# A pair's attention scores as two 64-row products, with the mask from a standing tile

## The chip, the cores and the metric

The kernel runs on one core of one Trainium2 chip. The time is device microseconds of one execution, the median of three runs: 210.06 us before the change (209.74 to 210.12). Everything said about single instructions comes from one profiled execution.

## What is computed

Block-sparse attention over 4 batches, 8 heads, 768 positions and 64 features, followed by a gated MLP with a spatial product. The change touches the attention alone:

```python
scores = scale * np.matmul(q, k.transpose(0, 1, 3, 2))
...
scores = np.where(mask, scores, -1000000000.0)
scores = scores - np.max(scores, axis=-1, keepdims=True)
attn = np.exp(scores)
attn = attn / (np.sum(attn, axis=-1, keepdims=True) + 1e-09)
return np.matmul(attn, v).astype(np.float32)
```

The mask is one 768 x 768 pattern of 32 x 32 blocks, the same for all heads and batches: a band, the first and last block of rows and columns, and three sampled blocks for each block of rows.

## The kernel before

Heads are worked on in pairs: a batch has four pairs, the kernel 16 (`p`). A pair's keys and queries are cast to bf16 by GpSimd (`nat`), and a DMA transpose on SP's queue (`tr_dma`, L372) turns them into `tt`, 128 partitions by 12 blocks of 128 columns: partitions 0 to 63 hold the features of the pair's first head, 64 to 127 those of its second; the first six blocks are keys, the other six queries. The first batch (pairs 0 to 3) is transposed on TensorE instead and has its own functions.

`kq` (L83) has a row of 2 x 768 columns for each of eight heads. Its partitions 0 to 63 are that head's keys and queries. Its partitions 64 to 127 are the mask, written once: on the key side a one-hot of the key's block, on the query side 0 for an allowed block and -300 for a forbidden one. One product over all 128 partitions therefore gives score plus mask. VectorE copies each head of `tt` into its row of `kq` (`split`, L376), two copies for a pair.

From batch 1 on, the work goes by slots. A unit `j` is one head; it has six slots, one for each chunk `ci` of 128 keys. In a slot `qk_full` (L422) makes the scores of 128 keys by all 768 queries in two matmuls (512 and 256 columns) into one of two score buffers of PSUM (`sc`, two banks each), and ScalarE writes their exponential into `a_all`. Seven slots later (`LAG`) `av_full` (L471) multiplies: for one chunk `qc` of 128 queries, six matmuls of 65 columns over the six chunks of keys; the 65th column is the sum. When a unit's six are done, VectorE normalises it into `xn` (`normalize`, L438). In between, each slot takes some steps of the MLP off a queue (`run_queue`): matmuls of up to 512 columns into two single PSUM banks (`moeA`, `moeB`), read by VectorE or ScalarE. The order on each engine is the order in which the program issues; the slot lists `at`, `pre` and `late` say what else is issued in a slot, and the main loop (L846) runs scores, `pre`, value products, `at`, MLP steps, `late`. Slots 0 to 35 (`S0` = 36) are the first batch, slots 36 to 179 the 24 units of the other three.

Before the loop, `mask_rows` (L268) makes the mask's query side with a product of `bm`, in one case over partitions 64 to 87 alone; the matmuls of `filler` (L177) stand around it.

Of the kernel before, what the change touches and what calls it, by code (L numbers as in the profile page):

```python
# [10 lines left out]
FP32 = mybir.dt.float32  # L11
BF16 = mybir.dt.bfloat16
I32 = mybir.dt.int32
AF = mybir.ActivationFunctionType
ALU = mybir.AluOpType
# [11 lines left out]
def kernel(  # L27
# [16 lines left out]
    nc = tc.nc  # L44

    B, H, S, D = q.shape
# [3 lines left out]
    NCH = S // 128  # L50
# [6 lines left out]
    NG = H // 2  # L57
# [13 lines left out]
    work = ctx.enter_context(tc.tile_pool(name="work", bufs=1))  # L71
    psum = ctx.enter_context(tc.tile_pool(name="psum", bufs=1, space=bass.MemoryType.PSUM))
# [10 lines left out]
    kq = const.tile([128, H, 2 * S], BF16, name="kq")  # L83
# [2 lines left out]
    MR = slice(D, KR)  # L86
    MX = slice(D, 128)
    K_, Q_ = slice(0, S), slice(S, 2 * S)

    def qcols(t0, n=1):  # L90
        return slice(S + t0 * TW, S + (t0 + n) * TW)
# [91 lines left out]
    def ts(out, in0, s1, o0, s2=None, o1=None):  # L183
        kw = {} if o1 is None else {"op1": o1}
        nc.vector.tensor_scalar(out=out, in0=in0, scalar1=s1, scalar2=s2, op0=o0, **kw)  # L185

    def tt_op(out, in0, in1, op):
        nc.vector.tensor_tensor(out=out, in0=in0, in1=in1, op=op)
# [21 lines left out]
    def dve_copy(o, i):  # L210
        nc.vector.tensor_copy(out=o, in_=i)  # L211
# [158 lines left out]
    tt = {}  # L370

    def tr_dma(p):  # L372
        tt[p] = work.tile([128, 2 * NCH, 128], BF16, tag="tt", bufs=2, name="tt")
        nc.sync.dma_start_transpose(out=tt[p], in_=nat.pop(p).rearrange("p c h d -> p (c h d)"))

    def split(p, h):  # L376
        src = tt[p].rearrange("x c n -> x (c n)")
        dve_copy(kq[0:D, (2 * p + h) % H, :], src[h * D:(h + 1) * D, :])


    a_ref, av_ref, x_ref, xn_ref, xt_ref = {}, {}, {}, {}, {}

# [4 lines left out]
    def qk_unit(u, e):  # L387
# [31 lines left out]
            ps = ps.rearrange("p (c n) -> p c n", c=len(parts))  # L419
        nc.scalar.activation(out=out, in_=ps, func=AF.Exp, scale=0.125)  # L420

    def qk_full(j, ci):  # L422
        if ci == 0:
            a_ref["h", j] = work.tile([128, NCH * S], BF16, tag="a_all", bufs=3,
                                      name="a_all").rearrange("p (c n) -> p c n", c=NCH)
        ps = psum.tile([128, 1024], FP32, tag="sc", bufs=2)
        for n0, n1 in ((0, 512), (512, S)):
            nc.tensor.matmul(out=ps[:, n0:n1],  # L428
                             lhsT=kq[:, j % H, ci * 128:(ci + 1) * 128],
                             rhs=kq[:, j % H, S + n0:S + n1], start=True, stop=True)  # L430
        nc.scalar.activation(out=a_ref["h", j][:, ci, :], in_=ps[:, 0:S], func=AF.Exp, scale=0.125)  # L431

    def av_tile(key, n):
        ps = psum.tile([128, 512], FP32, tag="av", bufs=2, name="ps_av")
        av_ref[key] = ps[:, 0:n * VA].rearrange("p (c d) -> p c d", d=VA)
        x_ref[key] = ps[:, 512 - TW // 2:512].bitcast(BF16)

    def normalize(ps, out, n):  # L438
        rc = work.tile([128, NCH, 1], FP32, tag="rc", bufs=2)
        nc.vector.reciprocal(out=rc[:, 0:n], in_=ps[:, :, D:VA])  # L440
        nc.vector.tensor_tensor(out=out, in0=ps[:, :, 0:D],  # L441
                                in1=rc[:, 0:n].to_broadcast([128, n, D]), op=ALU.mult)

    def av_unit(u, e):
        t, p = UNITS[u]
        if e == 0:
            av_tile(u, 2 * TC)
        for i in range(8 * e, 8 * e + 8):
            g, ci = divmod(i, NCH)
            if t == "h":  # L450
                h, qc, to, n = p, g, g, 2 * TC
                pp = 0
            else:
                (h, qc), n, pp = divmod(g, TC), TC, p
                to = qc * 2 + h
            at = (h * NCH + ci) * n * 128 if t != "h" else ci * n * 128
            at += qc * 128
            nc.tensor.matmul(out=av_ref[u][:, to, :], lhsT=a_ref[u][:, at:at + 128],  # L458
                             rhs=vv[pp % NVV][:, h, ci, :],
                             start=(ci == 0), stop=(ci == NCH - 1))  # L460
        if e == 2:
            a_ref.pop(u)
            if t == "h":
                if p == 0:
                    xn_ref[0] = work.tile([128, 2 * TC, 2, D], BF16, tag="xn0", bufs=1, name="xn0")
                normalize(av_ref.pop(u), xn_ref[0][:, :, p, :], 2 * TC)
            else:
                xn_ref[u] = work.tile([128, TC, 2, D], BF16, tag="xn3", bufs=3, name="xn3")
                normalize(av_ref.pop(u), xn_ref[u].rearrange("p c h d -> p (c h) d"), 2 * TC)

    def av_full(j, qc):  # L471
        p, h = divmod(j, 2)
        if qc == 0:
            av_tile(j, NCH)
        for ci in range(NCH):
            nc.tensor.matmul(out=av_ref[j][:, qc, :],  # L476
                             lhsT=a_ref["h", j][:, ci, qc * 128:(qc + 1) * 128],
                             rhs=vv[p % NVV][:, h, ci, :],
                             start=(ci == 0), stop=(ci == NCH - 1))
        if qc == NCH - 1:  # L480
            a_ref.pop(("h", j))
            if h == 0:
                xn_ref["p", p] = work.tile([128, NCH, 2, D], BF16, tag="xn", bufs=2, name="xn")
            normalize(av_ref.pop(j), xn_ref["p", p][:, :, h, :], NCH)

    def xt_tile(p):
        if p not in xt_ref:
# [224 lines left out]
    def run_queue():  # L712
        if not queue or pace["slots"] <= 0:
            return
        pace["credit"] += (len(queue) - pace["credit"]) / pace["slots"]
        pace["slots"] -= 1
        n = int(pace["credit"] + 0.5)
        for _ in range(min(n, len(queue))):
            queue.popleft()()
            pace["credit"] -= 1  # L720
# [3 lines left out]
    at, late, pre = {}, {}, {}  # L724

    def when(slot, *fns):
        at.setdefault(slot, []).extend(fns)

    def c(f, *a, **kw):
        return lambda: f(*a, **kw)  # L730
# [77 lines left out]
    def slot_of(p):  # L808
        return S0 + 12 * (p - NG)

    for p in range(NG, NP):
        g = slot_of(p)
        when({4: 14, 5: 20, 6: 28, 11: g - 29, 15: g - 29}.get(p, g - 36), c(load, p, "k"), c(load, p, "q"), c(load, p, "v"))
        when({4: 17, 5: 23, 6: 37, 11: g - 22, 15: g - 22}.get(p, g - 24),
             *[c(cast, p, nm, PL, cs=cs) for nm in "kqv" for cs in (((C01, C23, C45) if p > 5 else (ALLC,)))])
        when({4: 21, 5: 27, 11: g - 18, 15: g - 18, 10: g - 17, 14: g - 17}.get(p, g - 19), c(tr_dma, p))
        if p % NG == 1 and p > 2 * NG:
            late.setdefault(g - 4, []).append(c(split, p, 0))
        else:
            when(g - 5, c(split, p, 0))  # L820
        when(g + 4 if p == NG else g - 3, c(split, p, 1))
        if p == NP - 1:
            when(g + 20, last_x)
        elif p % NG == NG - 1:
            when(g + 19, c(xtr_dma, p))
        else:
            when(g + 20, c(xtr_dma, p))
# [13 lines left out]
    for u in range(len(UNITS)):  # L841
        for e in range(3):
            sl = (5, 6, 6)[e] if u == 0 else 3 * u + e + (4 if u < 3 else 3)
            av_at.setdefault(sl, []).append((u, e))
    NS = S0 + 12 * (NP - NG)
    for s in range(NS + LAG + 2):  # L846
        if s < S0:
            qk_unit(*divmod(s, 3))
        elif s < NS:
            j, ci = divmod(s - S0, NCH)  # L850
            qk_full(j + H, ci)
        early = at.get(s, [])
        for f in pre.get(s, []):
            f()
        for u, e in av_at.get(s, []):
            av_unit(u, e)
        if 0 <= s - LAG - S0 and s - LAG < NS:
            j, qc = divmod(s - LAG - S0, NCH)
            av_full(j + H, qc)
        for f in early:  # L860
            f()
        run_queue()
        for f in late.get(s, []):
            f()
        while post:
            post.pop(0)()
# [31 lines left out]
```

## Time and profile before

| | |
|---|---|
| time, median of 3 runs | 210.06 us |
| span of the profiled execution | 208.3 us |
| TensorE, matmul busy | 201.0 us (97%) |
| TensorE, weight loads | 138.0 us (66%) |
| VectorE busy | 146.8 us (70%) |
| ScalarE busy | 168.4 us (81%) |
| GpSimd busy | 89.4 us (43%) |
| granted TensorE clock | 1.000 |

The span runs from the first to the last instruction of that execution; the time holds in addition what lies around it. PE is TensorE's matmuls, PEld its weight loads, DVE VectorE, ACT ScalarE, POOL GpSimd, SP the engine that issues the transfers. In a row of instruction groups stand the line, the engine, the operation, what is written and read with partitions x elements, the count, the busy time, the mean of one in ns, and the idle time of the engine just before, with what ended it. A row of the order of time has start, length (both us) and how many instructions are merged. Matmuls are pipelined: a row's length includes the way through the array, so the pace is read from the distance between starts.

### The profile page before, as it was taken

To read this page: it belongs to the slowest core of one execution; us is meant where nothing else is said; L and a number is where in the kernel's file an instruction comes from. 1 tells how busy PE (TensorE), PEld (TensorE's weight loads), DVE (VectorE), ACT (ScalarE), POOL (GpSimd) and SP (SyncE) were. 2 spreads that over 40 slices of the span, in tenths; PEclk is the share of its full clock that TensorE was granted. 3 is DMA by queue.
4 is the path that set the end of the run, shared out by engine and by line. 5 is a ranking of instruction groups with operands and counts; after the bars stand their busy time and mean duration, and the time that the engine had idled before them with its cause. 6 is when DMAs were issued, how large, how long until landed. Compare 5 with 4: busy or idle time off the path is not lost.

```text
span 208.3 us, 5489 instructions
## 1 busy us (share of the span) xinstructions
PE 201.0 (97%) x2203; PEld 138.0 (66%) x2225; DVE 146.8 (70%) x315; ACT 168.4 (81%) x222; POOL 89.4 (43%) x186
## 2 busy tenths in 40 slices
PE   6899999999999999999999999999999999999993
PEld 6599888777766776667556676667665567445551
DVE  6888776989876766575975585456875666576871
ACT  6899999999999999989899878889899884266021
POOL 6888989767927964006757600006210000013000
PEclk9999999999999999999999999999999999999999
DMA  5999899999999999499987920499402010610016
GB/s 143 338 362 357 275 383 270 206 247 389 253 253 308 259 300 208 139 199 386 292 176 206 139 41 0 164 189 335 75 0 41 0 37 4 250 57 0 0 70 232
DMA packets 53053, 39.48 MB, mean 190 GB/s; under 512 B 33956, under 2 KB 47652, under 8 KB 53028
## 3 DMA queue, kind: packets, MB, share of 16 engines
q1 hardware_dynamic: 52596, 38.74, 70.0%
q10 hardware_dynamic: 432, 0.39, 0.6%
q8 instruction: 17, 0.28, 0.5%
q14 instruction: 8, 0.07, 0.1%
HBM read 24.77 MB, written 6.29 MB: 149 GB/s over the span
## 4 chain that ended last, share of the span: by engine, by line
PE 87%; DVE 4%; ACT 4%; DMA 2%; issue 1%; POOL 0%; ACTq 0%
PE ps L428 21%; PE ps_moe L630 17%; PE ps_moe L561 13%; PE ps_av L476 12%; PE ps L415 7%; PE ps_av L458 4%; PE ps_t L561 4%; PE ps_t L630 4%; PE ps_sc L630 2%; ACT a_all L420 2%; DVE stats L594 2%; DVE vn L185 2%; DMA st_q<-in_q_dram 2%; PE ps_sc L561 1%; PE ps L263 1%
## 5 line engine op out<-in xcount | busy, mean ns | idle before, releaser
L431 ACT ACTIVATE a_all<-ps 128x768 bf16<-128x768 f32 x144 | 113.4, 812 | 13.8 <-PE ps L428 6.2
L428 PE MATMUL ps<-kq 128*128 128x512 bf16 (+1 forms) x288 | 70.3, 326 | 0.3
L476 PEld LDWEIGHTS <-a_all 128*128 128x128 bf16 x864 | 46.6, 98 | 19.0
L476 PE MATMUL ps_av<-vv,a_all 128*128 128x65 bf16 x864 | 51.1, 194 | 0.1
L428 PEld LDWEIGHTS <-kq 128*128 128x128 bf16 x288 | 27.9, 97 | 23.6
L137 POOL CAST nat<-st_k 128x256 bf16<-128x256 f32 (+3 forms) x37 | 17.7, 509 | 38.7 <-DMA st_k<-in_k_dram 38.7
L420 ACT ACTIVATE a_all<-ps 128x1024 bf16<-128x1024 f32 x35 | 33.5, 1027 | 0.3
L630 PE MATMUL ps_moe<-w_spt,vn 128*128 128x512 bf16 (+1 forms) x144 | 33.1, 325 | 0.0
L598 POOL TENSOR_SCALAR std<-mv 128x3 f32<-128x3 f32 (+1 forms) x9 | 3.4, 376 | 48.7 <-DVE mv L595 48.5
L661 DVE TENSOR_TENSOR sb<-ps_moe,b_row 128x512 f32<-128x512 f32 x18 | 12.4, 690 | 14.5 <-PE ps_moe L630 14.2
L630 PE MATMUL ps_moe<-xt,w_in_t 128*128 128x256 bf16 (+1 forms) x108 | 21.7, 299 | 0.2
L415 PE MATMUL ps<-kq 128*128 128x256 bf16 x135 | 20.8, 275 | 0.8 <-DVE kq L211 0.6
L561 PE MATMUL ps_moe<-w_in_t,xt 128*128 128x512 bf16 x65 | 20.2, 378 | 0.2
L137 POOL CAST vv<-st_v 128x256 bf16<-128x256 f32 (+2 forms) x37 | 18.5, 533 | 3.9 <-DMA st_v<-in_v_dram 3.8
L137 POOL CAST nat<-st_q 128x256 bf16<-128x256 f32 (+2 forms) x41 | 19.2, 496 | 1.6 <-DMA st_q<-in_q_dram 1.5
L561 PE MATMUL ps_moe<-w_out_t,un 128*128 128x512 bf16 x64 | 19.4, 378 | 0.2
L441 DVE TENSOR_TENSOR xn<-ps_av,rc 128x384 bf16<-128x384 f32 (+1 forms) x36 | 18.5, 513 | 1.4 <-DVE rc L440 0.2
L664 DVE TENSOR_TENSOR un<-sb,un 128x512 bf16<-128x512 f32 x24 | 17.4, 727 | 1.5
L630 PEld LDWEIGHTS <-vn 128*128 128x128 bf16 x192 | 15.5, 97 | 4.4
L594 DVE BATCH_NORM_STATS2 stats<-vn 128x6 f32<-128x512 bf16 x24 | 16.5, 688 | 1.5 <-ACT vn L589 0.9
L211 DVE COPY osb<-ps_moe 128x512 f32<-128x512 f32 x12 | 8.3, 689 | 11.2 <-PE ps_moe L561 9.3
L211 DVE COPY kq<-tt 64x1536 bf16<-64x1536 bf16 x24 | 15.4, 641 | 0.6 <-DMA tt<-nat 0.2
(94 smaller groups left out, 241.6 us busy)
## 6 DMA issues: line engine op xcount, KB each, us to landing
out_dram<-osb SPq DMA_DIRECT2D x23, 256.0 KB, 2.1
st_k<-in_k_dram SPq DMA_DIRECT2D x15, 384.0 KB, 4.6
st_v<-in_v_dram SPq DMA_DIRECT2D x15, 384.0 KB, 6.2
st_q<-in_q_dram SPq DMA_DIRECT2D x12, 384.0 KB, 4.9
ws_f<-in_moe_w_spatial_dram SPq DMA_DIRECT2D x6, 384.0 KB, 5.5
w_f<-in_moe_w_in_dram SPq DMA_DIRECT2D x8, 256.0 KB, 6.3
w_f<-in_moe_w_out_dram SPq DMA_DIRECT2D x4, 256.0 KB, 5.4
st_q<-in_q_dram SPq DMA_DIRECT2D x3, 256.0 KB, 6.9
```

Of the source, the lines that this page charges most:

```text
L137: eng.tensor_copy(out=dst, in_=src)
L211: nc.vector.tensor_copy(out=o, in_=i)
L415: nc.tensor.matmul(out=ps[:, at:at + n * TW], lhsT=kq[:, h, ci * 128:(ci + 1) * 128], rhs=kq[:, h, qcols(t0, n)], start=True, stop=True)
L420: nc.scalar.activation(out=out, in_=ps, func=AF.Exp, scale=0.125)
L428: nc.tensor.matmul(out=ps[:, n0:n1], lhsT=kq[:, j % H, ci * 128:(ci + 1) * 128], rhs=kq[:, j % H, S + n0:S + n1], start=True, stop=True)
L431: nc.scalar.activation(out=a_ref["h", j][:, ci, :], in_=ps[:, 0:S], func=AF.Exp, scale=0.125)
L441: nc.vector.tensor_tensor(out=out, in0=ps[:, :, 0:D], in1=rc[:, 0:n].to_broadcast([128, n, D]), op=ALU.mult)
L476: nc.tensor.matmul(out=av_ref[j][:, qc, :], lhsT=a_ref["h", j][:, ci, qc * 128:(qc + 1) * 128], rhs=vv[p % NVV][:, h, ci, :], start=(ci == ...
L561: nc.tensor.matmul(out=ref["ps"][:, 0:w], lhsT=lhs(i), rhs=rhs(i), start=(i == 0), stop=(i == n - 1))
L594: nc.vector.bn_stats(out=stats, in_=self.vn[:, tcc, :])
L630: nc.tensor.matmul(out=o.rearrange("p (c t) -> p c t", c=n), lhsT=lhs(i)[:, (d0 + x) * 128:(d0 + x + 1) * 128], rhs=rhs(i), start=(i == 0) ...
L664: nc.vector.tensor_tensor(out=self.in_place(*area), in0=sb, in1=self.in_place(*area), op=ALU.mult)
```

## The change

A unit `j` is no longer one head with all queries but a pair `p` with half `f` of the queries, 384 of them. For a chunk of 128 keys the two heads' scores are two products, each over 64 partitions, straight from `tt`: partitions 0 to 63 into the first bank of the score buffer, 64 to 127 into the second. The copies of `split` are gone. From pair 6 on, `tt` is not a tile of its own but row 4 + (p - 2) % 4 of `kq`.

The mask comes in two ways. For four chunks of keys (0, 2, 4, 5) two more 64-row products add it to the scores in PSUM, from row 0 of `kq`, whose lower half `mask_low` fills with a copy of its upper half. For chunks 1 and 3 (`DVE_MASKED`) the exponential is taken of the plain scores, and VectorE then takes the minimum with `keep`, which is 0 where the mask forbids and 3e38 where it allows. `keep` stands in rows 1 to 3 of `kq`; `mask_chunk` makes two of its chunks in slots 30 and 31, by a pair of 64-row products and a comparison.

```diff
+    keep = kq[:, 1:4].rearrange("p h n -> p (h n)").rearrange("p (c n) -> p c n", c=NCH)
+    TOP = 3.0e38
...
     def tr_dma(p):
-        tt[p] = work.tile([128, 2 * NCH, 128], BF16, tag="tt", bufs=2, name="tt")
+        if p < NG + 2:
+            tt[p] = work.tile([128, 2 * NCH, 128], BF16, tag="tt", bufs=2, name="tt")
+        else:
+            tt[p] = kq[:, 4 + (p - 2) % 4].rearrange("x (c n) -> x c n", n=128)
...
-    def split(p, h):
-        src = tt[p].rearrange("x c n -> x (c n)")
-        dve_copy(kq[0:D, (2 * p + h) % H, :], src[h * D:(h + 1) * D, :])
...
+    DVE_MASKED = (1, 3)
+    HW = S // 2
+
+    def mask_low():
+        dve_copy(kq[0:D, 0, :], kq[MX, 0, :])
+
+    def mask_chunk(ci):
+        ps = psum.tile([128, 1024], FP32, tag="sc", bufs=2, name="ps_m").rearrange("p (h n) -> p h n", h=2)[:, :, 0:HW]
+        for f in range(2):
+            r = slice(f * D, (f + 1) * D)
+            nc.tensor.matmul(out=ps[:, f], lhsT=kq[r, 0, ci * 128:(ci + 1) * 128],
+                             rhs=kq[r, 0, S + f * HW:S + (f + 1) * HW], start=True, stop=True)
+        ts(keep[:, ci].rearrange("p (f n) -> p f n", f=2), ps, -1.0, ALU.is_ge, TOP, ALU.mult)
+
     def qk_full(j, ci):
+        p, f = divmod(j, 2)
...
-        ps = psum.tile([128, 1024], FP32, tag="sc", bufs=2)
-        for n0, n1 in ((0, 512), (512, S)):
-            nc.tensor.matmul(out=ps[:, n0:n1],
-                             lhsT=kq[:, j % H, ci * 128:(ci + 1) * 128],
-                             rhs=kq[:, j % H, S + n0:S + n1], start=True, stop=True)
-        nc.scalar.activation(out=a_ref["h", j][:, ci, :], in_=ps[:, 0:S], func=AF.Exp, scale=0.125)
+        ps = psum.tile([128, 1024], FP32, tag="sc", bufs=2, name="ps_s").rearrange("p (h n) -> p h n", h=2)[:, :, 0:HW]
+        by_dve = ci in DVE_MASKED
+        for h in range(2):
+            r = slice(h * D, (h + 1) * D)
+            nc.tensor.matmul(out=ps[:, h], lhsT=tt[p][r, ci], rhs=tt[p][r, NCH + f * TW3:NCH + (f + 1) * TW3],
+                             start=True, stop=by_dve)
+        if not by_dve:
+            for h in range(2):
+                r = slice(h * D, (h + 1) * D)
+                nc.tensor.matmul(out=ps[:, h], lhsT=kq[r, 0, ci * 128:(ci + 1) * 128],
+                                 rhs=kq[r, 0, S + f * HW:S + (f + 1) * HW], start=False, stop=True)
+        a = a_ref["h", j][:, ci]
+        nc.scalar.activation(out=a, in_=ps, func=AF.Exp, scale=0.125)
+        if by_dve:
+            masks.append(lambda: tt_op(a, a, keep[:, ci:ci + 1, f * HW:(f + 1) * HW].to_broadcast([128, 2, HW]), ALU.min))
...
     def av_full(j, qc):
...
-                             lhsT=a_ref["h", j][:, ci, qc * 128:(qc + 1) * 128],
+                             lhsT=a_ref["h", j][:, ci, h, ql * 128:(ql + 1) * 128],
...
+    when(30, mask_low)
+    for i, ci in enumerate(DVE_MASKED):
+        late.setdefault(30 + i, []).append(c(mask_chunk, ci))
...
             av_full(j + H, qc)
+        while masks:
+            masks.pop(0)()
```

`av_full` takes the value products of a unit by half of the queries and by head (`ql, h = divmod(qc, 2)`); their number and size stay. The order of the DMA issues, of the casts on GpSimd and of the exponentials on ScalarE stays as it was.

More of the change, by code (lines that the diff above doesn't have):

```diff
@@ L422, in qk_full @@
     def qk_full(j, ci):
+        p, f = divmod(j, 2)
         if ci == 0:
             a_ref["h", j] = work.tile([128, NCH * S], BF16, tag="a_all", bufs=3,
-                                      name="a_all").rearrange("p (c n) -> p c n", c=NCH)
-        ps = psum.tile([128, 1024], FP32, tag="sc", bufs=2)
-        for n0, n1 in ((0, 512), (512, S)):
-            nc.tensor.matmul(out=ps[:, n0:n1],
-                             lhsT=kq[:, j % H, ci * 128:(ci + 1) * 128],
-                             rhs=kq[:, j % H, S + n0:S + n1], start=True, stop=True)
@@ L431, in qk_full @@
-        nc.scalar.activation(out=a_ref["h", j][:, ci, :], in_=ps[:, 0:S], func=AF.Exp, scale=0.125)
+                                      name="a_all").rearrange("p (c h n) -> p c h n", c=NCH, h=2)
+        ps = psum.tile([128, 1024], FP32, tag="sc", bufs=2, name="ps_s").rearrange("p (h n) -> p h n", h=2)[:, :, 0:HW]
[4 more added lines that the diff above has]
+                             start=True, stop=by_dve)
@@ L433, in av_tile @@
+        if ci == NCH - 1 and f == 1:
+            tt.pop(p)
+    masks = []
+    TW3 = NCH // 2
     def av_tile(key, n):
@@ L471, in av_full @@
     def av_full(j, qc):
-        p, h = divmod(j, 2)
+        p, f = divmod(j, 2)
+        ql, h = divmod(qc, 2)
         if qc == 0:
@@ L481, in av_full @@
             a_ref.pop(("h", j))
-            if h == 0:
+            if f == 0:
                 xn_ref["p", p] = work.tile([128, NCH, 2, D], BF16, tag="xn", bufs=2, name="xn")
-            normalize(av_ref.pop(j), xn_ref["p", p][:, :, h, :], NCH)
+            normalize(av_ref.pop(j), xn_ref["p", p][:, f * TW3:(f + 1) * TW3].rearrange("p c h d -> p (c h) d"), NCH)
     def xt_tile(p):
@@ L816 @@
         when({4: 21, 5: 27, 11: g - 18, 15: g - 18, 10: g - 17, 14: g - 17}.get(p, g - 19), c(tr_dma, p))
[L817 to L821, printed above, removed]
         if p == NP - 1:
```

## Prediction

> **What bounds the kernel now.** I read the shares of busy time first, then the chain of work that ended last, then the costliest groups.
>
> ```profile
> span 208.3 us, 5489 instructions
> PE 201.0 (97%) x2203; PEld 138.0 (66%) x2225; DVE 146.8 (70%) x315; ACT 168.4 (81%) x222; POOL 89.4 (43%) x186
> ...
> PE 87%; DVE 4%; ACT 4%; DMA 2%; issue 1%; POOL 0%; ACTq 0%
> ...
> L431 ACT ACTIVATE a_all<-ps 128x768 bf16<-128x768 f32 x144 | 113.4, 812 | 13.8 <-PE ps L428 6.2
> L428 PE MATMUL ps<-kq 128*128 128x512 bf16 (+1 forms) x288 | 70.3, 326 | 0.3
> ```
>
> TensorE is busy 97% of the span and is 87% of the chain. A busy matmul row includes the end of its pipeline, so the 97% alone proves little; the 0.3 us of idle time before 288 score matmuls says more: TensorE practically never waits. Next I asked for the busy time in the stretch where the changed function runs (first score matmul of L428 to the last exponential), and in the part of it where VectorE is fullest.
>
> ```profile
> core 0: us, PE busy (x) PEld busy (x) DVE busy (x) ACT busy (x) POOL busy (x), PEclk, DMA share, GB/s
> 40.30:173.00 132.70, 131.95 (x1456) 87.74 (x1469) 92.18 (x181) 119.02 (x159) 51.74 (x113) 1.00 0.75 185
> ...
> 36.00:52.00 16.00, 15.89 (x191) 11.69 (x190) 14.67 (x33) 15.22 (x19) 11.73 (x23) 1.00 1.12 284
> ```
>
> 144 chunks (24 units of six) take 132.7 us, 0.92 us each. TensorE sets this pace; ScalarE with 119.0 us is 13.7 us behind it, VectorE with 92.2 us further. What TensorE gains or loses per chunk is therefore gained or lost at the end, down to ScalarE's floor. The third view is the order of time on TensorE and its weight loads, to see what one chunk is made of.
>
> ```profile
> 104.18 0.38 PE L561 MATMUL ps_moe<-w_in_t,xt 128*128 128x512 bf16 x1
> 104.39 0.49 PE L428 MATMUL ps<-kq 128*128 128x512 bf16 x2
> 104.72 0.35 PE L476 MATMUL ps_av<-vv,a_all 128*128 128x65 bf16 x6
> 104.91 0.59 PE L561 MATMUL ps_moe<-w_in_t,xt 128*128 128x512 bf16 x2
> 105.34 0.49 PE L428 MATMUL ps<-kq 128*128 128x512 bf16 x2
> ...
> 104.18 0.31 PEld L428 LDWEIGHTS <-kq 128*128 128x128 bf16 x2
> ```
>
> Read starts, not lengths. Two 512-column matmuls go from 104.91 to 105.34: 0.215 us each, 0.42 ns a column. The scores (512 + 256 columns) hold TensorE for 0.32 us, the six value products for 0.19 us, 0.032 us each. The first score weights were loaded from 104.18 on, beside the matmul before: loads cost nothing here as long as they may run ahead.
>
> **The change on TensorE, columns.** A chunk had 768 columns on the whole array. Now it has a pair of 64-row products of 384 columns each, one on partitions 0 to 63, one on 64 to 127, into two banks of PSUM; four chunks of six have a second such pair for the mask. No row of this trace shows two matmuls at once, so the pair is bounded: at best both halves stream together, 384 columns, 0.16 us; at worst one after the other, 0.32 us. I take together, because the two share no partition, no row of the array and no bank, with the second product starting half of the 0.032 us pitch later (0 to 0.032). An unmasked chunk then takes 0.16 + 0.016 instead of 0.32 us, −0.145; a chunk with mask 0.32 + 0.016, +0.016. A unit: 2 × −0.145 + 4 × 0.016 = −0.226 us; 24 units: **−5.4 us** (−7.7 with no offset, −3.1 with 0.032; one after the other, 0 for two chunks and +0.32 for four, +31 us). The Trainium skill, "TensorE: Matmul & The Clock Gate", section "The mechanism" of part 3, says that matmuls on different row groups run at the same time, about 4 ns apart; by that the term would be −7.1 us, and no run here shows it.
>
> **The change on TensorE, going between whole array and half.** The stream around each score pair stays on 128 rows. The trace has one matmul that uses less than half of the rows, the mask product of L269 with 24 rows at partition 64:
>
> ```profile
> 5.14 0.28 PE L179 MATMUL wps<-warm 128*128 128x128 bf16 x2
> ...
> 5.19 0.22 PE L179 MATMUL wps<-warm 128*128 128x128 bf16 x1
> 5.34 0.28 PE L269 MATMUL mq<-kq,bm 24*128 24x256 bf16 x1
> ...
> 5.08 0.15 PEld L179 LDWEIGHTS <-warm 128*128 128x128 bf16 x2
> 5.34 0.09 PEld L269 LDWEIGHTS <-bm 24*128 24x128 bf16 x1
> ...
> 3.46 0.84 ACT L214 ACTIVATE kq<-kq 64x768 bf16<-64x768 bf16 x1
> 3.74 0.17 DVE L185 TENSOR_SCALAR bm<-allow 24x24 bf16<-24x24 f32 x1
> ```
>
> The two fillers ahead of it start at 5.14 and 5.19, 0.055 us apart, so the next matmul was due at 5.25. It started at 5.34, and its weight load, which elsewhere starts beside the matmul before, started at 5.34 too, though `bm` had been ready since 3.91 and the mask columns that the matmul reads since 4.30. So 0.09 us of empty array lies ahead of the 24-row product. I read it as the price of going from 128 rows to fewer: the load is not let ahead until the array is empty. What the way back costs the trace can't show, since the load after it waits for VectorE. Bounds for a way: 0 (something else delayed that one load) and 0.09; I take 0.09 in and, because the same load-ahead is lost, 0.09 out. Two ways a chunk, 144 chunks: 288 × 0.09 = **+25.9 us** (0 to 25.9; 13.0 if one way only). Between the two pairs of a chunk with mask the row count stays, and I put nothing. The Trainium skill, "TensorEngine Tiling (Array Packing)", section "Key Properties", says that a change of the tiling mode drains TensorE while a change of tile within a mode does not; the 0.09 us row agrees for the way in, and the way out no run here shows.
>
> **Building the standing tile.** At slots 30 and 31 two chunks of mask scores (a 64-row pair each) and two VectorE operations from PSUM, behind one copy of 64 × 1536.
>
> ```profile
> 28.00:32.00 4.00, 4.00 (x69) 3.72 (x67) 2.78 (x10) 3.92 (x5) 3.73 (x7) 1.00 1.05 385
> ...
> L441 DVE TENSOR_TENSOR xn<-ps_av,rc 128x384 bf16<-128x384 f32 x24 | 13.4, 558 | 1.0 <-DVE rc L440 0.2
> L441 DVE TENSOR_TENSOR xn<-ps_av,rc 128x256 bf16<-128x256 f32 x12 | 5.1, 424 | 0.4
> L185 DVE TENSOR_SCALAR vn<-ps_moe 128x512 bf16<-128x512 f32 x18 | 12.4, 687 | 4.2 <-PE ps_moe L561 3.8 <-PE ps L428 0.3
> ```
>
> TensorE and ScalarE are both full there. Each chunk costs TensorE 0.176 + 0.18 = 0.36 us, 0.7 us together. It also takes one of the two score buffers, so the next scores go without double buffering, and the buffer comes free only after VectorE's read. From PSUM, 128 more columns cost VectorE 134 ns (558 − 424), so 768 columns take 0.687 + 256 × 1.05 ns = 0.95 us. Bounds: 0.7 us, and 0.7 + 2 × 0.95 = 2.6 us if nothing hides the reads; VectorE has 1.2 of the 4 us free, so I take **+1.2 us**.
>
> **VectorE.**
>
> ```profile
> L211 DVE COPY kq<-tt 64x1536 bf16<-64x1536 bf16 x24 | 15.4, 641 | 0.6 <-DMA tt<-nat 0.2
> ...
> L188 DVE TENSOR_TENSOR kq<-hot,lim 64x768 bf16<-64x768 bf16 x1 | 0.6, 555 | 0.0
> ```
>
> The 24 split copies go (−15.4 us), 48 minima of 768 bf16 columns come. The nearest row is the 64x768 bf16 operation of two tensors, 555 ns; the upper bound is the 0.95 us just worked out for a source in PSUM. 48 × 0.555 = 26.6 us (45.6 at most). With the copy (0.64) and the two reads (1.9), VectorE gains 13.8 us (32.8), of 208.3 − 146.8 = 61.5 us that are free. On the path: nothing. The minimum waits for its exponential, and behind it in VectorE's order stand the reads of the two `moe` banks and the normalisation; a bank is needed again only after a whole product in the other, four 0.215 us steps and the chunks between them. The value products need chunk 3 masked four slots later, 3.7 us, against 0.81 for the exponential and 0.56 for the minimum. Without that cover, each late read costs up to 0.81 us. On ScalarE the same 768 columns stay 0.81 us.
>
> **Moved buffers.** The transposes on SP's queue keep their place and size; from pair 6 on they land in freed rows of `kq`, four slots instead of two. Score weights now wait for the landing itself; the transposes are issued 15 to 21 slots (13 us and more) ahead, and VectorE's total wait for them was 0.2 us. I put nothing.
>
> **Sum.** −5.4 + 25.9 + 1.2 = +21.7 us on the profiled span of 208.3 us: 230.0 us. The median of the runs, 210.06, is 1.8 us above that span, which holds what lies outside of it; I carry it over: **231.8 us**. Own range, with 0.075 to 0.1 us a way and the offset's bounds: 226 to 237.
>
> **The rivals.** (A) is the forecast. (B) *No gap*: the late load at 5.34 had a cause of its own, and the pairs stream together. Then −5.4 on the columns and +0.8 for the standing tile. For it: one row only speaks of the gap, with 24 rows and not 64. Against it: I find nothing else that load could have waited for. ScalarE's floor of 119 us in 132.7 allows it, but in 36 to 52 us ScalarE (15.22 of 16) and VectorE (14.67) leave almost no room, so about 1 us is lost: 210.06 − 3.6 = 206.5 us (203 to 209). This is the other side, faster; it decides when a way costs under (5.4 − 1.2) / 288 = 0.015 us. (C) *One way, or half price*: 13.0 us instead of 25.9: +8.8, 218.9 us (213 to 226). For it: leaving the half array may let the next load ahead, since the half has its own weights; nothing in the trace excludes it. (D) *The pair does not run together*, so the change doesn't do what it says: +31 on the columns, 242 us without gaps, 268 with them. For it: no two matmuls overlap anywhere in the trace. (E) *VectorE becomes the bound* with no gap: minima at 0.95 us bring 36 to 52 us above its 16 us (14.67 + 2 per unit × 0.95 − 2 × 0.641 per pair), and late `moe` banks stall TensorE there and at each exponential: +2 to +8 us, about 214.
>
> **How the numbers follow.** (A) 0.45, (C) 0.26, (B) 0.17, (D) 0.07, (E) 0.05. The time is (A)'s. The range leaves out (B) and the half of (D) with gaps, 0.2 together: 211 to 246 us. A change under 0.2% can't be told from none here; only the edges of (B), (C) and (E) reach it: faster 0.17, same 0.03, slower 0.80.
>
> **What would show it.** Right: on TensorE some 0.09 us of extra distance ahead of each score pair and behind it, weight loads of the pair starting with their matmul, chunks at about 1.07 us, ScalarE waiting for scores far more often. The second product starting within 0.03 us of the first confirms the columns' term; a distance of 0.16 us is (D). Weight loads that start during the value products before them, and a chunk at 0.87 us, are (B). Loads late on one side only are (C). VectorE at 100% between 36 and 52 us with TensorE waiting for it is (E). The forecast is wrong if the gap is a matter of the 24 rows or of that one place.

## The result and the profile after

| | before | after |
|---|---|---|
| time, median (4 runs each) | 210.09 us | 234.97 us |
| range of the runs | 209.74 to 210.5 | 234.76 to 235.9 |
| span of the profiled execution | 208.3 us | 233.2 us |

The ratio is 1.119 (95% interval 1.117 to 1.122): 24.9 us slower, against a forecast of 21.7; the forecast time was 231.8 us, with a range of its own of 226 to 237. The page of the kernel after, the lines that answer to those of before:

```profile
span 233.2 us, 5902 instructions
...
PE 224.6 (96%) x2398; PEld 116.1 (50%) x2421; DVE 161.9 (69%) x342; ACT 171.8 (74%) x222; POOL 88.9 (38%) x186
...
PE 92%; DVE 3%; ACT 3%; issue 1%; ACTq 0%
...
L453 ACT ACTIVATE a_all<-ps_s 128x768 bf16<-128x768 f32 x144 | 116.1, 811 | 32.8 <-PE ps_s L450 24.4
...
L190 DVE TENSOR_TENSOR a_all<-a_all,kq 128x768 bf16<-128x768 bf16 x48 | 28.2, 588 | 22.8 <-ACT a_all L453 22.8
L445 PE MATMUL ps_s<-kq 64*128 64x384 bf16 x240 | 40.3, 333 | 0.6
...
L445 PEld LDWEIGHTS <-kq 64*128 64x128 bf16 x240 | 11.5, 92 | 42.6 <-issue 42.6
L450 PE MATMUL ps_s<-kq 64*128 64x384 bf16 x192 | 31.3, 323 | 0.0
```

Three things can be read here. ScalarE's exponentials are as long as before (811 ns) but wait 32.8 us instead of 13.8, most of it for the products of L450: ScalarE has moved further away from the bound. TensorE is still busy 96%: the busy share hides what happened. The row that gives it away is that of the weight loads: those of L445 stood idle 42.6 us for nothing that the profile shows ("issue"). And 240 matmuls of 333 ns make a busy time of 40.3 us: 120 pairs of 336 ns. The two products of a pair lie almost entirely on top of each other.

The same in order of time, on TensorE and its weight loads, an unmasked chunk (at 123.16) and one with mask products (at 122.00):

```profile
121.47 0.59 PE L660 MATMUL ps_moe<-xt,w_in_t 128*128 128x512 bf16 x2
122.00 0.34 PE L445 MATMUL ps_s<-kq 64*128 64x384 bf16 x2
122.17 0.33 PE L450 MATMUL ps_s<-kq 64*128 64x384 bf16 x2
122.43 0.36 PE L506 MATMUL ps_av<-vv,a_all 128*128 128x65 bf16 x6
...
122.64 0.59 PE L660 MATMUL ps_moe<-xt,w_in_t 128*128 128x512 bf16 x2
123.16 0.34 PE L445 MATMUL ps_s<-kq 64*128 64x384 bf16 x2
123.43 0.37 PE L506 MATMUL ps_av<-vv,a_all 128*128 128x65 bf16 x6
...
122.61 0.13 PEld L660 LDWEIGHTS <-w_in_t 128*128 128x128 bf16 x2
123.16 0.10 PEld L445 LDWEIGHTS <-kq 64*128 64x128 bf16 x2 [0.42 <-issue]
123.43 0.24 PEld L506 LDWEIGHTS <-a_all 128*128 128x128 bf16 x6 [0.17 <-issue]
```

Two 512-column matmuls from 122.64 are through at 123.07 (2 x 0.215); the pair starts at 123.16, 0.09 us late, and its weights are loaded only then. The pair's 0.16 us are over at 123.32; the value products start at 123.43, 0.1 us late, and their weights too are loaded only then. Between the pair of L445 and that of L450 there is no such gap: 0.17 us from start to start, 0.16 of them columns.

To see where the 24.9 us are, the span is cut at the first and the last score matmul (first and last start, from the view of one line; before, then after):

```profile
L428 PE MATMUL ps<-kq x288: 270/324/379, 40.3 to 172.8; 128*128 128x512 bf16 x144
```

```profile
L445 PE MATMUL ps_s<-tt x48: 332/333/333, 42.7 to 64.7; 64*128 64x384 bf16 x48
...
L450 PE MATMUL ps_s<-kq x192: 322/323/323, 42.8 to 197.6; 64*128 64x384 bf16 x192
```

Up to the first scores 42.7 instead of 40.3: +2.3 (with more digits), the standing tile. The 144 chunks 154.9 instead of 132.5: +22.4. The rest 35.6 instead of 35.5.

### The profile page after: what moved, and what is told of

Read it like the earlier page. It is cut to its first block, busy times and chain, and to the rows that moved or that the text cites. A ratio compares the mean times of both kernels' runs of the same rounds, so it can differ in the third digit from the quotient of the medians.

```text
span 233.2 us, 5902 instructions
## 1 busy us (share of the span) xinstructions
PE 224.6 (96%) x2398; PEld 116.1 (50%) x2421; DVE 161.9 (69%) x342; ACT 171.8 (74%) x222; POOL 88.9 (38%) x186
## 4 chain that ended last, share of the span: by engine, by line
PE 92%; DVE 3%; ACT 3%; issue 1%; ACTq 0%
PE ps_av L506 18%; PE ps_s L445 17%; PE ps_moe L660 17%; PE ps_moe L591 12%; PE ps_s L450 7%; PE ps L415 5%; PE ps_t L591 4%; PE ps_av L487 3%; PE ps_t L660 3%; PE ps_sc L660 2%; ACT a_all L420 2%; PE wps L181 2%; DVE vn L187 1%; PE ps_sc L591 1%; PE ps L265 1%
## 5 line engine op out<-in xcount | busy, mean ns | idle before, releaser
L453 ACT ACTIVATE a_all<-ps_s 128x768 bf16<-128x768 f32 x144 | 116.1, 811 | 32.8 <-PE ps_s L450 24.4
L506 PEld LDWEIGHTS <-a_all 128*128 128x128 bf16 x864 | 35.4, 98 | 38.1 <-issue 36.7
L506 PE MATMUL ps_av<-vv,a_all 128*128 128x65 bf16 x864 | 52.5, 196 | 0.1
L190 DVE TENSOR_TENSOR a_all<-a_all,kq 128x768 bf16<-128x768 bf16 x48 | 28.2, 588 | 22.8 <-ACT a_all L453 22.8
L445 PE MATMUL ps_s<-kq 64*128 64x384 bf16 x240 | 40.3, 333 | 0.6
L139 POOL CAST nat<-st_k 128x256 bf16<-128x256 f32 (+3 forms) x37 | 17.2, 496 | 56.1 <-DMA st_k<-in_k_dram 56.1
L445 PEld LDWEIGHTS <-kq 64*128 64x128 bf16 x240 | 11.5, 92 | 42.6 <-issue 42.6
L450 PE MATMUL ps_s<-kq 64*128 64x384 bf16 x192 | 31.3, 323 | 0.0
L628 POOL TENSOR_SCALAR std<-mv 128x3 f32<-128x3 f32 (+1 forms) x9 | 2.6, 286 | 62.3 <-DVE mv L625 60.0
```

What stands on the lines that cost most here:

```text
L139: eng.tensor_copy(out=dst, in_=src)
L445: nc.tensor.matmul(out=ps[:, h], lhsT=tt[p][r, ci], rhs=tt[p][r, NCH + f * TW3:NCH + (f + 1) * TW3], start=True, stop=by_dve)
L450: nc.tensor.matmul(out=ps[:, h], lhsT=kq[r, 0, ci * 128:(ci + 1) * 128], rhs=kq[r, 0, S + f * HW:S + (f + 1) * HW], start=False, stop=True)
L453: nc.scalar.activation(out=a, in_=ps, func=AF.Exp, scale=0.125)
L506: nc.tensor.matmul(out=av_ref[j][:, qc, :], lhsT=a_ref["h", j][:, ci, h, ql * 128:(ql + 1) * 128], rhs=vv[p % NVV][:, h, ci, :], start=(ci ...
```

## The experiments

### The price of a passage, by itself

The theory: at each passage, that is, each change between products on the whole array and products on half of its rows, no columns run for about 0.1 us, and this, twice a chunk, is the loss. The rivals: the loss is the mask products; the price is paid one way only; it belongs to an instruction more in that place. Four runs put one small product into each of the 144 chunks of the kernel *before*, ahead of the scores, into columns of the score buffer that nobody reads, on 128, 96, 64 or 32 rows. Nothing of the change is in them.

```diff
     def qk_full(j, ci):
...
         ps = psum.tile([128, 1024], FP32, tag="sc", bufs=2)
+        nc.tensor.matmul(out=ps[:, 992:1024], lhsT=warm[0:64], rhs=warm[0:64, 0:32], start=True, stop=True)
```

128 rows:

> The kernel before, with one small extra product of 32 columns on all 128 rows ahead of each of the 144 score pairs of slots 36 to 179 (its result is not used). Theory (each passage between whole and half array costs about 0.095 us): no passage here, only 144 x 0.013 to 0.032 us of TensorE, 212 to 215 us. Rival (what costs is an extra instruction and its weight load in that place): as slow as the next run.

64 rows:

> The same extra product on 64 rows instead of 128, otherwise the kernel before; no pair, no second mask product, no minimum. Theory: two passages for each of 144 chunks, 288 x 0.095 = 27 us more than the run with 128 rows, 239 to 243 us. Rival (the passage is paid on the way in alone): 13.7 us more, 226 to 229 us. Rival (no price of passage; the changed kernel is slow for its mask products): within 1 us of the run with 128 rows.

32 rows:

> The kernel before with the small extra product of 32 columns on 32 rows. Theory (the price is that of changing how the rows are divided, however few): as on 64 rows, 241 to 243 us. Rival (fewer rows empty sooner, or the array's division into four costs more): a difference of more than 2 us.

96 rows:

> The same on 96 rows. Theory (more than 64 rows is the whole array): as on 128 rows, 213 to 215 us. Rival (any product on fewer than 128 rows pays): 241 to 243 us.

| rows of the extra product | 128 | 96 | 64 | 32 |
|---|---|---|---|---|
| time, us | 213.74 | 214.40 | 242.28 | 242.06 |

Going from 96 to 64 rows costs 28 us at the same number of instructions and columns. 242.28 - 213.74 = 28.5 us over 288 passages is 0.099 us each. All three rivals fall: an extra instruction costs 0.025 us (3.64 / 144), one way only would have been half, and there are no mask products here. The trace of the run with 64 rows has both ways side by side, on TensorE:

```profile
120.70 0.59 PE L562 MATMUL ps_moe<-w_in_t,xt 128*128 128x512 bf16 x2
121.23 0.19 PE L427 MATMUL ps<-warm 64*128 64x32 bf16 x1
121.35 0.50 PE L429 MATMUL ps<-kq 128*128 128x512 bf16 x2
```

and of the run with 128 rows:

```profile
121.35 0.81 PE L631 MATMUL ps_moe<-w_spt,vn 128*128 128x512 bf16 x3
121.99 0.18 PE L427 MATMUL ps<-warm 128*128 128x32 bf16 x1
122.02 0.48 PE L429 MATMUL ps<-kq 128*128 128x512 bf16 x2
```

With 64 rows: due at 120.70 + 0.43 = 121.13, started at 121.23, and 0.12 us to the next start. With 128 rows: due at 121.35 + 0.645 = 121.995, started at 121.99, 0.03 us to the next. So a passage costs 0.1 us on the way in and 0.09 on the way out (0.12 less the 0.03 that the small product takes with 128 rows). What the array does in that time no view shows. By the profile's records it is not the load of the new weights itself: in the changed kernel that load starts only at the end of the gap, together with its product (both at 123.16).

### Half the passages

The scores of two chunks in one slot, one straight after the other, none in the next slot. Every product and minimum stays; 144 passages go.

```diff
-            qk_full(j + H, ci)
+            if ci % 2 == 0:
+                qk_full(j + H, ci)
+                qk_full(j + H, ci + 1)
```

> The changed kernel with the scores of two chunks issued in one slot, one straight after the other, and none in the next: 72 x 2 passages between whole and half array instead of 144 x 2, all products and minima stay. Theory: 144 x 0.099 = 14.3 us less than the changed kernel, 220 to 222 us. Rival (the gap belongs to each first pair of a chunk, because its score buffer or its weights come late): no gain, 233 us or more; two chunks at once also take both score buffers, which could cost up to some us.

Measured: 223.45 us (ratio to before 1.063, 1.061 to 1.065), 11.5 us under the changed kernel. Passages are worth time in the changed kernel itself, as the theory has it; the amount is 2.8 us short of 14.3. TensorE of this run:

```profile
121.21 0.59 PE L660 MATMUL ps_moe<-w_spt,vn 128*128 128x512 bf16 x2
121.74 0.34 PE L445 MATMUL ps_s<-kq 64*128 64x384 bf16 x2
121.91 0.33 PE L450 MATMUL ps_s<-kq 64*128 64x384 bf16 x2
122.07 0.33 PE L445 MATMUL ps_s<-kq 64*128 64x384 bf16 x2
122.23 0.33 PE L450 MATMUL ps_s<-kq 64*128 64x384 bf16 x2
122.49 0.36 PE L506 MATMUL ps_av<-vv,a_all 128*128 128x65 bf16 x6
```

Four pairs follow each other at 0.16 to 0.17 us, one gap before (121.64 to 121.74) and one behind (122.39 to 122.49). From the first to the last score matmul the 144 chunks gain 12.2 us; the first scores start 0.5 us later than in the changed kernel (43.2 against 42.7), and the rest behind the last is 0.6 us longer (36.2 against 35.6). What the chunks lack to 14.3 us, the trace shows at the score buffers. In 14 of the 72 slots the first pair of the second chunk starts 0.03 to 0.30 us late, 2.1 us in all, and each time it starts 0.05 us after the end of the exponential that read the same score buffer two chunks earlier. One such place, on TensorE and ScalarE:

```profile
67.26 0.33 PE L450 MATMUL ps_s<-kq 64*128 64x384 bf16 x2
67.72 0.34 PE L445 MATMUL ps_s<-kq 64*128 64x384 bf16 x2
...
66.87 0.80 ACT L453 ACTIVATE a_all<-ps_s 128x768 bf16<-128x768 f32 x1
```

The pair was due at 67.26 + 0.16 = 67.42; the exponential ends at 67.67, and the pair starts at 67.72. So 14.3 - 2.1 = 12.2 us: two chunks at once take both score buffers, and what the expectation put as a possible loss of some us is 2.1.

### What the mask products and the minima cost

```diff
-                             start=True, stop=by_dve)
-        if not by_dve:
+                             start=True, stop=True)
+        if False:
```

> The changed kernel without the 64-row mask products: chunks 0, 2, 4 and 5 go unmasked, the passages stay. Theory: 96 pairs of 0.164 to 0.174 us go, 235.0 - 16 = 219 us, still 9 us slower than before although two thirds of the score columns are gone. Rival (the mask products, and not the passages, are what the change costs): at or below the kernel before, 203 to 210 us.

Measured: 220.52 us, 14.5 us less, and 10.4 us over the kernel before. The expectation had 16 us. From the first to the last pair of L445 the chunks gain 15.0 (139.7 against 154.7 us); the first scores start 1.1 us later in this execution (43.8 against 42.7), though nothing ahead of them was changed. The scores' columns take half the time that they took in the kernel before (144 x 384 instead of 144 x 768; the expectation's two thirds is wrong), and it is still slower. The rival, that the mask products and not the passages are the loss, falls: they are 14.5 of the 24.9 us, and without them 10.4 are left.

```diff
-            masks.append(lambda: tt_op(a, a, keep[:, ci:ci + 1, f * HW:(f + 1) * HW].to_broadcast([128, 2, HW]), ALU.min))
+            pass
```

> The changed kernel without VectorE's 48 minima: chunks 1 and 3 go unmasked. Theory (VectorE is off the path): 234 to 236 us, as the changed kernel. Rival (value products wait for the minimum, or the minima hold up the reads of the MLP banks): 3 us or more below it.

Measured: 235.02 us. So the 28.2 us of VectorE's minima cost no time here, nor does their wait of 22.8 us for the exponentials.

### The standing tile

The run without minima, in addition without `mask_chunk` in slots 30 and 31:

```diff
-    for i, ci in enumerate(DVE_MASKED):
-        late.setdefault(30 + i, []).append(c(mask_chunk, ci))
```

> The changed kernel without minima and without the standing tile (no products and no reads for it in slots 30 and 31): chunks 1 and 3 go unmasked. Theory (building it holds up the score buffers there, which the trace puts at 2.3 us): 232.5 to 233 us, against 235.0 with the tile built and unused. Rival (the building is hidden and the 2.3 us come from elsewhere in the first stage): 235 us.

Measured: 232.89 us, 2.1 us under the run without minima. Its first scores start at 40.7 us, those of the run without minima at 42.5. What holds it up, on TensorE and VectorE of the changed kernel:

```profile
36.01 0.34 PE L432 MATMUL ps_m<-kq 64*128 64x384 bf16 x2 [0.76 <-DVE kq L213]
36.28 0.61 PE L415 MATMUL ps<-kq 128*128 128x256 bf16 x4
...
37.90 0.34 PE L432 MATMUL ps_m<-kq 64*128 64x384 bf16 x2 [0.32 <-DVE kq L187]
38.17 0.61 PE L415 MATMUL ps<-kq 128*128 128x256 bf16 x4
...
39.52 0.27 PE L415 MATMUL ps<-kq 128*128 128x256 bf16 x1 [0.27 <-DVE kq L187]
...
35.31 0.65 DVE L213 COPY kq<-kq 64x1536 bf16<-64x1536 bf16 x1
35.99 0.80 DVE L187 TENSOR_SCALAR vn<-vn,mv,rstd 128x512 bf16<-128x512 bf16 x1
36.71 0.27 DVE L213 COPY xt<-ps_av 128x256 bf16<-128x256 bf16 x1
36.91 0.94 DVE L187 TENSOR_SCALAR kq<-ps_m 128x768 bf16<-128x768 f32 x1
```

TensorE waits three times for VectorE: 0.76 us for the copy that fills the lower half of the mask's row, 0.32 and 0.27 us for a score buffer that VectorE has still to read. VectorE's rows stand end to end there. The three waits are 1.35 us together; with the 0.7 us of the two pairs and their passages, as forecast, this is about the 2.1 us measured.

### Both products of a pair on the same rows

To price what the pair's running together is worth: both products of each pair on partitions 0 to 63, into their two banks as before.

```diff
-            r = slice(h * D, (h + 1) * D)
+            r = slice(0, D)
...
-                r = slice(h * D, (h + 1) * D)
+                r = slice(0, D)
```

> The changed kernel with both products of every 64-row pair on partitions 0 to 63 (the second head's scores are not computed, the first head's come twice; the mask is the same on both halves). Theory (the pair streams together only because its halves of the array differ): 240 pairs, each 0.15 to 0.16 us longer, 36 to 38 us, 271 to 273 us. Rival (the two products would share the columns' time whatever their rows): 235 us.

Measured: 273.84 us, 38.9 us over the changed kernel, 0.162 us for each of the 240 pairs: the time of 384 columns. This is just above the expected 0.15 to 0.16 us a pair and 271 to 273 us. TensorE:

```profile
140.40 0.49 PE L445 MATMUL ps_s<-kq 64*128 64x384 bf16 x2
140.73 0.48 PE L450 MATMUL ps_s<-kq 64*128 64x384 bf16 x2
141.15 0.36 PE L506 MATMUL ps_av<-vv,a_all 128*128 128x65 bf16 x6
```

Four products of 384 columns, at 0.16 us each. On different rows the two products of a pair had taken the time of one.

### Is there a faster version of this kind?

Two chunks at once, and no mask at all (no mask products, minima or standing tile), as a floor:

> Two chunks at once and no mask at all: no mask products, no minima, no standing tile; all six chunks go unmasked. It is the floor of what 64-row pairs could give with free masks. Theory, from the sum of the single terms (grouped 223.4, mask products -14.5, building -2.1): 206 to 208 us, about 3 us under the kernel before. Rival (ScalarE's floor or the score buffers take the rest): 209 us or more, no version of this kind can beat the kernel before.

Measured: 207.36 us, ratio 0.985 (0.982 to 0.989) to its own runs of the kernel before, 210.31: 2.9 us under it. The terms of columns and passages alone, 144 passages at 0.099 us less 144 chunks at 0.160, would be -8.8 us. Most of what lies between is again the wait for a score buffer: in this trace the second chunk starts late in 30 of the 72 slots, 5.3 us in all, each time 0.05 us after the end of the exponential that read its buffer. So the run gives the floor with two score buffers, not that of the pairs as such.

A version that also masks has to pay for it out of these 2.9 us, and out of 8.8 even if the buffers cost nothing. The mask products cost 14.5. With minima on all six chunks, the standing tile alone, at 2.1 us for two chunks where it is built now, takes most of the 2.9, and VectorE would get 144 x 0.588 = 85 us on top of the 134.5 of this run, 219 us in all. By this estimate no version with these two kinds of mask beats the kernel before; besides the changed kernel and the run with two chunks at once (223.45 us), none was measured.

## Why the prediction was right, point by point

**The bound.** TensorE set the pace of the chunks before, and what a chunk lost there was lost at the end: +22.4 of 24.9 us lie between the first and the last score matmul, and both ScalarE and VectorE are idle longer than before (61.4 and 71.3 us of the span, instead of 39.9 and 61.5).

**The columns.** Forecast -5.4 us (-7.7 to -3.1). The offset of a pair's second product is 3 ns (336 against 333 ns) and not 16, and the mask pair starts 0.173 us after the first: an unmasked chunk has 0.163 instead of 0.323 us, a chunk with mask 0.173 + 0.163 = 0.336. (2 x -0.160 + 4 x 0.013) x 24 = -6.4 us. That the pair streams together, which the forecast took from the code alone, is shown by the pair's rows and by the run on the same rows. The Trainium skill ("TensorE: Matmul & The Clock Gate", "The mechanism") gives starts about 4 ns apart; the trace agrees, with 3 ns.

**The passages.** Forecast +25.9 us, from one matmul of 24 rows. The mechanism, both ways and the size hold: 0.099 us from the pair of runs on 64 and 128 rows, x 288 = +28.5 us. With the columns this makes +22.1 us, the trace has +22.4. The row of the 24-row product was read with two decimals as 0.09 (the trace's third decimal makes it 0.096); 288 x 0.009 = 2.6 us is most of the 3.2 us that the forecast lacks. The Trainium skill ("TensorEngine Tiling (Array Packing)", "Key Properties") says that a change of the tiling mode, not of the tile alone, drains TensorE; the traces agree, with 0.1 us each way, and with pairs that follow each other at 0.16 to 0.17 us without such a gap.

**The standing tile.** Forecast +1.2 (0.7 to 2.6), measured 2.1 by the runs and 2.3 by the first start. This term was mis-sized, inside its bounds. I read VectorE's free time from 28 to 32 us, but slots 30 and 31 lie at 35 to 38 us, where VectorE is full, so nothing hid its reads; and I counted the copy of `mask_low` as VectorE's time only, though the product behind it waits for it (0.76 us). The +1.2 was a choice between the bounds: 2.6 us less the 1.2 that VectorE was thought to have free would have been 1.4.

**The sum.** With measured sizes the three terms are -6.4 + 28.5 + 2.1 = +24.2 of the 24.9 us; 0.7 us stay unassigned. The columns came out better than forecast and the two costs worse, so their errors cancel in part. The range's lower edge is, by its own terms, 288 x 0.075 - 7.7 + 1.2 = +15.1 us, that is 225 us and not 226; nothing hangs on it.

**VectorE.** The minimum takes 588 ns, forecast 555. It is off the path, as the run without it shows.

**The rivals.** No gap (B) falls: the weights are loaded at the pair, not ahead of it, and the passages cost 28.5 us. One way only (C) falls: the rows show a gap on both ways. Not together (D) falls: that would be the 273.84 us of the run on the same rows. VectorE as the bound (E) falls: taking the minima away changes nothing.

## What to carry to other kernels

Two products on half of the rows each do run at once, but each way between whole and half array costs what some 235 columns cost here (0.099 us at 0.42 ns). Count the passages before the columns: a lone pair of 384 columns saves 0.16 us and pays 0.2. It can pay where several such pairs stand together (two chunks of unmasked pairs at once came out 2.9 us under the kernel before) or, by the same count, where nothing on more than 64 rows lies in between, which no run here tried. And when the rows that an operand leaves free already carry something, as the mask did here, splitting has to buy that back too: 14.5 us for the mask products.

## What was not expected

- 96 rows cost no passage (214.40 us against 213.74 with 128), and 32 rows cost the same as 64 (242.06 and 242.28): what counts here is whether more than 64 rows are used.
- TensorE's busy share does not show the gaps: 97% before, 96% after, with 28.5 us in it in which no columns run, because a matmul's row reaches 0.16 us past its columns (two rows of 0.43 us of columns last 0.59). The idle time of the weight loads with no releaser (42.6 us at L445) shows them.
- The 38.9 us lost with both products on the same rows are the columns' time and no more, so loading new weights for rows that are in use costs nothing there: the next product starts 0.16 us after the one before, the time of its columns.
